# Hash products read in a permuted column order, three VectorE steps put elsewhere, and one more low part in 24 on GpSimd

## The chip, the cores and the metric

The kernel runs on one core of a Trainium2 chip. The metric is the time of one execution in microseconds (us). The engines are called as the profile calls them: PE is TensorE (PEld its weight loads), DVE is VectorE, ACT is ScalarE, POOL is GpSimd, SP is SyncE, which here only issues DMAs.

## The reference

There are 4 x 8 heads of 768 rows with 64 features. A row of q or k gets a hash of 6 bits (the signs of its products with `proj`), and a query attends only to keys with the same hash. The attention output, as 3072 rows of 512, goes through a layer of width 2048 with a piecewise quadratic activation.

```python
q_bits = (np.einsum('bhsd,dk->bhsk', q, proj) > 0)      # the same for k
mask = q_bucket[:, :, :, None] == k_bucket[:, :, None, :]
scores = np.where(mask, scale * q @ k.T, -1e9)
attn = softmax(scores)
x = (attn @ v)  ->  (3072, 512)
h = x @ w_in
g = where(h >= 1, h, where(h <= -1, 0, (h + 1)**2 / 4))
out = g @ w_out
```

## The kernel before

Everything is float32, and products are made from parts: a value is split into a high part (rounded for the matmul) and a low part, and the products of the parts are added up in PSUM. The attention (until about 442 us) runs over 384 units `g`, 12 to a head: two half heads (384 query columns each) of six blocks of 128 keys. Two heads make a pair of 24 units. In the text a unit is numbered 0 to 23 within its pair; units 0 to 11 are the even head, 12 to 23 the odd one. So the half heads of a pair are units 0 to 5, 6 to 11, 12 to 17 (the third half head) and 18 to 23.

Unit `g` is written out in the loop at L691 to L715, and each engine runs its share in that order:

- `s_unit(g)`: two matmuls (L437, L438) put the scores into one of four PSUM banks `s`; ACT writes the high part of the exponential to `ph` (L446) and the whole exponential either back to PSUM or to an SBUF tile `pf` (L451).
- `max_red` (L376): DVE reduces the row maxima whose products were made at the end of the unit before. There is one such pair of matmuls (L359, tile `smax`, one buffer) at the end of every even unit, so the reduction stands at the head of every odd unit, behind the scores.
- `lo_unit(g - 1)`: the low part `pl`, by POOL for key blocks 0 and 3 of a half head (`POOL_J`), by DVE for the other four (both print as L39, the line of `sub`).
- `pv_unit(g - 4)`: three matmuls (L471, L473 with `ph`, L475 with `pl`) add the unit's product with v to the bank `obank[hf]`. `PV_ORDER` says in which order the six blocks of a half head are taken; at the end of a half head ACT copies the bank out (`xs`, L481).
- then the tasks that were registered for unit `g`, in the order in which they were registered.

Three kinds of task matter here.

The hash bits of the pair two ahead: `bits_mm` makes four matmuls (L235) into `obank[1]`, and ACT writes the negated second half of them (`neg`, L241); `bits_cmp` (L246) is a DVE comparison that reads the bank and `neg`. For pairs 4 to 15 the first half is multiplied in unit 5 and compared in unit 6, the second half is multiplied in unit 7, into the same bank, and compared in unit 8. `bits_scale` (L305 on POOL, L303 on ACT for pairs 1 and 2) turns the flags into the values that are put into the operands, and `bits_put` (L314) issues four DMAs for them in unit 18.

The conversion of the weights (`WeightSplit.steps`), one block of 512 columns per head: `rebias` on ACT (L82) and `tail` on DVE (L86, which writes its word into `obank[0]`, free at that point), `shifted` on DVE (L90), `signed` on DVE (L94), which reads that word for the last time. Counted from the head in which the conversion begins they stand in units 9, 10, 11 and 14.

The maxima's way back: POOL clamps them (L403, L405), PE transposes them (L414).

`streamed` and `into` (L42, L47) are two views of eight columns at a time: a matmul that reads `streamed(x)` and writes `into(ps)` takes the eight columns in the order 0 4 1 5 2 6 3 7 and writes them one after the other. L437, L438, L359 and L471 to L475 do so; L235 reads and writes straight.

Of the kernel before, what the change touches and what calls it, by code (L numbers as in the profile page):

```python
# [11 lines left out]
F32 = mybir.dt.float32  # L12
# [10 lines left out]
P = 128  # L23
NH = B * H
NPAIR = NH // 2
NJ = S // P
HS = S // 2
# [14 lines left out]
def streamed(t):  # L42

    return t.rearrange("p (g r w) -> p g w r", r=2, w=4)


def into(t):  # L47
    return t.rearrange("p (g w r) -> p g w r", w=4, r=2)
# [71 lines left out]
NQK, NV, NP_ = 3, 2, 7  # L120
LAG = 4
POOL_J = (0, 3)
PV_ORDER = (1, 2, 0, 4, 5, 3)
NU = 2 * NJ
SHIFT = 4


def attention(ctx, tc, wst, T1, T2, qk, v, pj, cv, x_d, s_d, e_d, tasks, shared):
    nc = tc.nc
    const = ctx.enter_context(tc.tile_pool(name="aconst", bufs=1))  # L130
    work = ctx.enter_context(tc.tile_pool(name="awork", bufs=2))
# [28 lines left out]
    pw = const.tile([P, 3, P], F32R, name="pw")  # L160
# [68 lines left out]
    def bits_mm(pr, hf, bank):  # L229
        t1, t2 = T1[pr % NQK], T2[pr % NQK]  # L230
        sl = slice(hf * HS, (hf + 1) * HS)
        ps = obank[bank]
        for n in range(4):
            h, x = n // 2, (t2[:, 1], t1[:, 0])[n % 2]
            nc.tensor.matmul(out=ps[:, 0:HS], lhsT=pw[:, h, :], rhs=x[:, h, sl], start=(n == 0), stop=(n == 3))  # L235
        if hf == 0:
            bits_t[pr] = (small.tile([32, S], F32R, name="bits", bufs=1),
                          small.tile([32, S], F32, name="neg", bufs=1), {})
        bt, neg, pss = bits_t[pr]
        pss[hf] = ps  # L240
        nc.scalar.activation(out=neg[:, sl], in_=ps[32:64, 0:HS], func=AF.Copy, scale=-1.0)  # L241
# [56 lines left out]
    def bits_scale(pr, eng, hf=None):  # L298
        bt, neg, _ = bits_t[pr]
        if hf is not None:  # L300
            bt, neg = (t[:, hf * HS:(hf + 1) * HS] for t in (bt, neg))
        if eng is nc.scalar:
            eng.activation(out=bt, in_=neg, func=AF.Identity, scale=cvt[:, 0:1], bias=cvt[:, 1:2])  # L303
            return
        eng.tensor_scalar(out=bt, in0=neg, scalar1=cvt[:, 0:1], scalar2=cvt[:, 1:2],  # L305
                          op0=ALU.mult, op1=ALU.add)
# [118 lines left out]
    units = {}  # L425

    def pool_lo(g):
        return g % NJ in POOL_J

    def s_unit(g):  # L430
        hd, hf, j = g // NU, (g % NU) // NJ, g % NJ
        pr, h = hd // 2, hd % 2
        t1, t2 = T1[pr % NQK], T2[pr % NQK]
        sl = slice(hf * HS, (hf + 1) * HS)
        ks = slice(j * P, (j + 1) * P)
        ps = ps_s.tile([P, 512], F32, name="s")
        nc.tensor.matmul(out=into(ps[:, 0:HS]), lhsT=t1[:, 1, h, ks], rhs=streamed(t1[:, 0, h, sl]), start=True, stop=False)  # L437
        nc.tensor.matmul(out=into(ps[:, 0:HS]), lhsT=t2[:, 1, h, ks], rhs=streamed(t2[:, 0, h, sl]), start=False, stop=True)  # L438
        ph, pl = PH[g % NP_], PL[g % NP_]
        if hd >= NH - 2 and j == 4:  # L440
            pf = ps[:, 0:HS]
            nc.scalar.activation(out=pf, in_=pf, func=AF.Exp, scale=SCALE)
            nc.vector.tensor_copy(out=ph[:, 0:HS], in_=pf)
            units[g] = (pf, ph, pl)
            return
        nc.scalar.activation(out=ph[:, 0:HS], in_=ps[:, 0:HS], func=AF.Exp, scale=SCALE)  # L446
        if pool_lo(g):
            pf = work.tile([P, HS], F32, name="pf", bufs=2)
        else:
            pf = ps[:, 0:HS]  # L450
        nc.scalar.activation(out=pf, in_=ps[:, 0:HS], func=AF.Exp, scale=SCALE)  # L451
        units[g] = (pf, ph, pl)
# [7 lines left out]

    def pv_unit(n, between):
        hd, hf, jj = n // NU, (n % NU) // NJ, n % NJ
        j = PV_ORDER[jj]
        pr, h = hd // 2, hd % 2
        va, vb = VA[pr % NV], VB[pr % NV]
        _, ph, pl = units.pop(n - jj + j)
        o = obank[hf]
        w = HS if hf == 0 else HS + 8
        wa = va[:, j, h:h + 2, :].rearrange("p g d -> p (g d)")
        wb = vb[:, j, h:h + 2, :].rearrange("p g d -> p (g d)")  # L470
        nc.tensor.matmul(out=into(o[:, 0:w]), lhsT=wa, rhs=streamed(ph[:, 0:w]), start=(jj == 0), stop=False)  # L471
        between(3)
        nc.tensor.matmul(out=into(o[:, 0:w]), lhsT=wb, rhs=streamed(ph[:, 0:w]), start=False, stop=False)  # L473
        between(4)
        nc.tensor.matmul(out=into(o[:, 0:HS]), lhsT=wa, rhs=streamed(pl), start=False, stop=(jj == NJ - 1))  # L475
        if jj == NJ - 1:
            if hf == 0:
                xss[hd] = work.tile([P, S + 2], F32, name="xs")
            xs = xss[hd]
            w = HS if hf == 0 else HS + 2  # L480
            nc.scalar.copy(out=xs[:, hf * HS:hf * HS + w], in_=o[:, 0:w])  # L481
            if hf == 1:
                xss.pop(hd)
                rs, sr = 64 * h, 64 * (1 - h)
                nc.sync.dma_start(out=x_d[hd // H][rs:rs + 64, pr % (H // 2), :], in_=xs[rs:rs + 64])
                nc.sync.dma_start(out=s_d[hd // H][hd % H:hd % H + 1, :], in_=xs[sr:sr + 1, 0:S])
# [42 lines left out]
    def at(g, fn, *a):  # L529
        tasks[g].append((fn, a))  # L530

    first = [raw0(), raw0()]
    for hf in range(2):
        sl = slice(hf * HS, (hf + 1) * HS)
# [107 lines left out]
    for hd in range(NH):  # L642
        pr, h = hd // 2, hd % 2
        g = hd * NU
        if 0 < hd < NH - 2:
            gc, gt = ((30, 32), (41, 43))[hd - 1] if hd < 3 else (g + NU + SHIFT - 1, g + NU + SHIFT + 1)
            at(gc, max_clamp, hd + 2, nc.gpsimd)
            at(gt, max_tr, hd + 2)
            at(gt, max_put, hd + 2)
        if h == 0 and pr + 2 < NPAIR:  # L650
            g0 = g + (13, 2)[pr] if pr < 2 else g
            for n in range(4):
                gq = g0 + n + (pr == 1 and n == 3)
                at(gq, cast_h, pr + 2, nc.gpsimd, n % 2, n // 2)
                at(gq, low_h, pr + 2, nc.gpsimd, n % 2, n // 2)
            for n in range(2):
                at(g0 + 3 + (pr == 1), move, pr + 2, n)
            at(g0 + 6, move, pr + 2, 2)
            if pr + 3 < NPAIR:
                at(g0 + 7, load_raw, pr + 3)  # L660
            bits_at = (((20, 1), (22, 0)), ((8, 1), (11, 0)))[pr] if pr < 2 else ((5, 1), (7, 1))
            for hf, (n, bank) in enumerate(bits_at):
                at(g + n, bits_mm, pr + 2, hf, bank)
                at(g + n + 1, bits_cmp, pr + 2, hf)
            at(g + n + 1, move, pr + 2, 3)
            if pr:
                at(g + n + 2, bits_scale, pr + 2, nc.gpsimd)
            else:
                at(g + 22, bits_scale, 2, nc.scalar, 0)
                at(g + 24, bits_scale, 2, nc.scalar, 1)  # L670
            at(g + (18 if pr else 24), bits_put, pr + 2)
        if h == 0 and pr + 1 < NPAIR:
            gv = g + LAG + (2 if pr else 16)
            at(gv, cast_v, pr + 1, nc.scalar)
            at(gv + 1, split_v, pr + 1, nc.gpsimd, 0)
            at(gv + 3, split_v, pr + 1, nc.gpsimd, 1)
            if pr + 2 < NPAIR:
                at(gv + (6 if pr else 4), load_v, pr + 2)
# [7 lines left out]
    for i in range(2 * NJ):  # L686
        n = 5 * 31 + 35 * i // 4
# [500 lines left out]
def lsh_attn_ffn(ctx: ExitStack, tc: tile.TileContext, qk, v, pj, cv, w_in, w_out, out):  # L1188
    nc = tc.nc
# [42 lines left out]
    def at(g, fn, *a):  # L1232
        tasks[g].append((fn, a))

    def conv(g, steps, offs):
        for fn, n in zip(steps, offs):
            at(g + n, fn)
# [6 lines left out]
    def wi_steps(i, cp, stage=None):  # L1244
        return ws.steps(win_v[:, :, i * P:(i + 1) * P, :], (P, NCT, P, 2), wih[i], wil[i], cp, stage, None, wq[i], word)
# [4 lines left out]
    woh = [hi for hi, lo in wo]  # L1250
    wol = [lo for hi, lo in wo]
    for i in range(NW1):
        conv((2 * i + 3) * NU, wi_steps(i, nc.scalar), (0, 9, 10, 11, 14 - (i == 0), 17, 19, 21))
    g0 = (NH - 4) * NU
    late = {}
    for n in range(NSTG):
        i = n - (NFT - NW1)
        stage = wq[NW1 + n] if i < 0 else xdp.tile([P, DM], F32, name=f"wd{n}")
        if i < 0:
            first, late[n] = wi_steps(NW1 + n, nc.gpsimd, stage)  # L1260
        elif i < 2:
            first, late[n] = wo_steps(i, nc.gpsimd, stage)
        else:
            first, late[n] = wo_steps(i, nc.scalar, stage, nc.gpsimd if i < 4 else nc.vector)
        conv((4 + 2 * n) * NU, first, (0, 9, 10, 11, 14, 16))
    for n, g in enumerate((1, 7, 13, 25, 30, 35)):
        conv(g0 + g, late[n], (0, 5, 6))

# [1 line left out]
    for b in range(B - 1):  # L1270
        g = (b + 1) * H * NU + LAG + 4
# [32 lines left out]
    for i in range(2, NFT):  # L1304
        n = i + NFT - NW1
# [71 lines left out]
```

## Time and profile before

| | us |
|---|---|
| median of three runs | 926.28 (926.24 to 926.52) |
| the profiled execution, its own time | 929.79 |
| its span, first to last instruction | 927.4 |
| mean granted clock of PE | 0.997 |

The profile comes from one execution of its own, 3.5 us longer than the median; 2.4 us of its time lie outside the span. In the views a matmul is shown with its whole duration (326 ns for 384 columns), though the next one starts after about half of that, so a busy PE is not a PE that never waits. What PE loses is seen from the starts of its instructions in the timeline, and from what the weight load ahead of a matmul waited for (PEld in the list of waits). DVE and ACT instructions overlap the next one of their engine by some 0.1 us as well, so sums of durations can pass the length of a stretch.

### The profile page before, as it was taken

Reading aid. Unit: us, or ns where it says so; the run is one execution under the profiler, and the core shown is the slowest. Engines: PE = TensorE matmul, PEld = TensorE weight load, DVE = VectorE, ACT = ScalarE, POOL = GpSimd, SP = SyncE. Lnnn points to the kernel's source line nnn. Section 1 sums busy time; section 2 is a strip of 40 time slices with the busy share of each in tenths; the row PEclk is TensorE's granted clock in tenths of the full one; section 3 lists DMA queues with packets and bytes.
Section 4 is the critical chain, followed back from the end, with each engine's and each line's share of the span. In section 5 each row is a group of like instructions: output and inputs, shape, how many; then the busy total and the mean of one; then the engine's idle time right before and its main releaser. Section 6 shows DMA issues by size and latency. Waiting matters only on the chain.

```text
span 927.4 us, 15714 instructions
## 1 busy us (share of the span) xinstructions
PE 906.7 (98%) x5050; PEld 846.2 (91%) x5050; DVE 753.1 (81%) x1345; ACT 669.6 (72%) x1481; POOL 320.8 (35%) x428
## 2 busy tenths in 40 slices
PE   8999999999999999999999999999999999999997
PEld 7789999999999999999999998989999999999996
DVE  8878889988998899887798888788876778765564
ACT  7889998999989998998766565556565555554454
POOL 8867766667777666678100000000000000000000
PEclk9999999999999999999999999999999999999999
DMA  6776666776656666654496478976549564454431
GB/s 162 187 189 162 166 187 179 202 209 186 185 159 176 183 183 195 146 153 131 142 316 210 131 255 297 296 252 193 160 148 272 152 202 126 145 179 128 125 91 69
DMA packets 95691, 167.67 MB, mean 181 GB/s; under 512 B 14533, under 2 KB 52537, under 8 KB 95609
## 3 DMA queue, kind: packets, MB, share of 16 engines
q1 hardware_dynamic: 95344, 166.63, 62.4%
q8 instruction: 40, 0.66, 0.3%
q14 instruction: 43, 0.34, 0.1%
q10 hardware_dynamic: 264, 0.03, 0.0%
HBM read 106.13 MB, written 33.96 MB: 151 GB/s over the span
## 4 chain that ended last, share of the span: by engine, by line
PE 70%; ACT 10%; DMA 5%; DVE 5%; POOL 3%; issue 2%; SPq 1%; ACTq 0%; DVEq 0%; POOLq 0%
PE y L911 24%; PE h L1143 16%; PE h L1048 6%; PE smax L359 4%; PE s L437 4%; PE s L438 3%; PE o L475 3%; PE o L471 3%; PE o L473 3%; ACT ph L446 3%; ACT s L451 2%; PE o L235 2%; DVE nm L376 2%; DMA t<-bits 2%; DMA wq<-wsq 1%
## 5 line engine op out<-in xcount | busy, mean ns | idle before, releaser
L446 ACT ACTIVATE ph<-s 128x384 fp32r<-128x384 f32 x380 | 191.7, 504 | 32.6 <-PE s L438 30.7
L376 DVE TENSOR_REDUCE nm<-smax 128x1 f32<-128x768 f32 x168 | 159.7, 950 | 10.7 <-PE smax L359 9.1
L39 DVE TENSOR_TENSOR pl<-s,ph 128x384 fp32r<-128x384 f32 x256 | 137.8, 549 | 24.7 <-ACT s L451 19.3
L39 POOL TENSOR_TENSOR pl<-pf,ph 128x384 fp32r<-128x384 f32 x128 | 129.7, 1014 | 78.9 <-ACT pf L451 72.2
L876 DVE SCALAR_TENSOR_TENSOR t<-t 128x384 f32<-128x384 f32 x128 | 71.3, 557 | 87.3 <-ACT z L871 87.0
L451 ACT ACTIVATE s<-s 128x384 f32<-128x384 f32 x252 | 128.8, 511 | 0.0
L471 PE MATMUL o<-ph,va 128*128 128x392 f32 (+1 forms) x384 | 126.0, 328 | 0.7 <-DVE neg L246 0.7
L437 PE MATMUL s<-t 128*128 128x384 f32 x384 | 126.3, 329 | 0.0
L475 PE MATMUL o<-pl,va 128*128 128x384 f32 x384 | 125.4, 327 | 0.4 <-DVE pl L39 0.4
L473 PE MATMUL o<-ph,vb 128*128 128x392 f32 (+1 forms) x384 | 125.8, 328 | 0.0
L438 PE MATMUL s<-t 128*128 128x384 f32 x384 | 125.3, 326 | 0.1
L911 PE MATMUL y<-t,ghi 128*128 128x512 f32 x384 | 118.7, 381 | 2.0 <-ACT ghi L881 2.0
L359 PE MATMUL smax<-t 128*128 128x384 f32 x336 | 87.0, 341 | 6.0 <-DVE nm L376 4.3
L881 ACT CAST ghi<-z 128x384 fp32r<-128x384 f32 x129 | 64.9, 503 | 31.8 <-DVE z L877 31.4
L871 ACT ACTIVATE z<-t,m 128x384 f32<-128x384 f32 x128 | 78.7, 615 | 4.2
L911 PEld LDWEIGHTS y<-t,ghi 128*128 128x128 f32 x384 | 71.5, 190 | 8.8 <-ACT ghi L881 2.6
L1143 PE MATMUL h<-wbig,t 128*128 128x384 f32 x399 | 77.5, 329 | 0.3 <-DVE wsq L1162 0.3
L877 DVE TENSOR_TENSOR z<-t,z 128x384 f32<-128x384 f32 x128 | 71.4, 558 | 4.5
L911 PE MATMUL y<-woh,glo 128*128 128x512 f32 x192 | 73.1, 381 | 0.8 <-DVE glo L885 0.8
L870 ACT ACTIVATE t<-h,mh 128x384 f32<-128x384 f32 x56 | 32.5, 580 | 57.1 <-PE h L1048 33.7
L437 PEld LDWEIGHTS s<-t 128*128 128x128 f32 x384 | 72.5, 189 | 1.2
L475 PEld LDWEIGHTS o<-pl,va 128*128 128x128 f32 x384 | 72.6, 189 | 1.1 <-DVE pl L39 0.7
(207 smaller groups left out, 2029.8 us busy)
## 6 DMA issues: line engine op xcount, KB each, us to landing
t<-wc SPq DMA_DIRECT2D x92, 256.0 KB
t<-t SPq DMA_DIRECT2D x60, 384.0 KB
wraw<-wc SPq DMA_DIRECT2D x76, 256.0 KB
raw<-in_qk_dram SPq DMA_DIRECT2D x14, 768.0 KB
wraw<-in_w_in_dram SPq DMA_DIRECT2D x16, 512.0 KB
wraw<-in_w_out_dram SPq DMA_DIRECT2D x16, 512.0 KB
t<-ed SPq DMA_DIRECT2D x36, 192.0 KB
xd<-xs SPq DMA_DIRECT2D x32, 192.5 KB
```

The source lines that it names most:

```text
L39: eng.tensor_tensor(out=out, in0=a, in1=b, op=ALU.subtract)
L359: nc.tensor.matmul(out=into(ps[:, 0:HS]), lhsT=t2[:, 0, h, i * P:(i + 1) * P], rhs=streamed(t2[:, 1, h, hf * HS:(hf + 1) * HS]), start=Tru ...
L376: nc.vector.tensor_reduce(out=nmp(hd)[:, i:i + 1], in_=smax[hd][:, :, 0:HS], axis=AX.XY, op=ALU.max, negate=True)
L437: nc.tensor.matmul(out=into(ps[:, 0:HS]), lhsT=t1[:, 1, h, ks], rhs=streamed(t1[:, 0, h, sl]), start=True, stop=False)
L438: nc.tensor.matmul(out=into(ps[:, 0:HS]), lhsT=t2[:, 1, h, ks], rhs=streamed(t2[:, 0, h, sl]), start=False, stop=True)
L446: nc.scalar.activation(out=ph[:, 0:HS], in_=ps[:, 0:HS], func=AF.Exp, scale=SCALE)
L451: nc.scalar.activation(out=pf, in_=ps[:, 0:HS], func=AF.Exp, scale=SCALE)
L471: nc.tensor.matmul(out=into(o[:, 0:w]), lhsT=wa, rhs=streamed(ph[:, 0:w]), start=(jj == 0), stop=False)
L473: nc.tensor.matmul(out=into(o[:, 0:w]), lhsT=wb, rhs=streamed(ph[:, 0:w]), start=False, stop=False)
L475: nc.tensor.matmul(out=into(o[:, 0:HS]), lhsT=wa, rhs=streamed(pl), start=False, stop=(jj == NJ - 1))
L911: nc.tensor.matmul(out=into(ys[c][m]), lhsT=g_[:, m * P:(m + 1) * P], rhs=streamed(w), start=(first and k == 0), stop=(last and k == 2))
L1143: nc.tensor.matmul(out=into(ps), lhsT=w[:, cs], rhs=streamed(x), start=(n == 0 and s not in (2, 3, 6)), stop=(n == 5), skip_group_check=True)
```

## The change

It has six parts.

1. The hash products (L235) read `streamed` columns and write `into` the bank, so that the flags stand in permuted order; `bits_scale` puts them back: it reads `into(neg)` and writes `streamed(bt)`, with a step of four elements in what it writes.
2. For pairs 4 to 15, the first hash comparison is registered for unit 7 and no longer for unit 6. In unit 7 it stands behind that unit's reduction on DVE, and ahead of the second half's products on PE.
3. `signed` is registered one unit earlier (13 for 14), but for one block of `w_in` that keeps 14 and one that had 13. There it stands behind unit 13's or unit 1's reduction and ahead of the low part that it followed.
4. In the third half head of pairs 2 to 14 the low part of key block 5 goes to POOL too (`QUARTER_J`).
5. From unit 48 on (pair 2) the blocks of a half head are taken in the order 1 0 2 4 3 5 (`PV_LATER`).
6. `pf` has three buffers for two.

```diff
 POOL_J = (0, 3)
+FROM = 4 * 12
+QUARTER_J = ((0, 3), (0, 3), (0, 3, 5), (0, 3))
 PV_ORDER = (1, 2, 0, 4, 5, 3)
+PV_LATER = (1, 0, 2, 4, 3, 5)
 NU = 2 * NJ
...
         for n in range(4):
             h, x = n // 2, (t2[:, 1], t1[:, 0])[n % 2]
-            nc.tensor.matmul(out=ps[:, 0:HS], lhsT=pw[:, h, :], rhs=x[:, h, sl], start=(n == 0), stop=(n == 3))
+            nc.tensor.matmul(out=into(ps[:, 0:HS]), lhsT=pw[:, h, :], rhs=streamed(x[:, h, sl]), start=(n == 0),
+                             stop=(n == 3))
...
             bt, neg = (t[:, hf * HS:(hf + 1) * HS] for t in (bt, neg))
+        bt, neg = streamed(bt), into(neg)
         if eng is nc.scalar:
...
     def pool_lo(g):
-        return g % NJ in POOL_J
+        return g % NJ in (QUARTER_J[g // NJ % 4] if FROM <= g < (NH - 2) * NU else POOL_J)
...
         if pool_lo(g):
-            pf = work.tile([P, HS], F32, name="pf", bufs=2)
+            pf = work.tile([P, HS], F32, name="pf", bufs=3)
...
-        j = PV_ORDER[jj]
+        j = (PV_LATER if n >= FROM else PV_ORDER)[jj]
...
             for hf, (n, bank) in enumerate(bits_at):
                 at(g + n, bits_mm, pr + 2, hf, bank)
-                at(g + n + 1, bits_cmp, pr + 2, hf)
+                at(g + n + 1 + (pr > 1 and hf == 0), bits_cmp, pr + 2, hf)
...
     for i in range(NW1):
-        conv((2 * i + 3) * NU, wi_steps(i, nc.scalar), (0, 9, 10, 11, 14 - (i == 0), 17, 19, 21))
+        conv((2 * i + 3) * NU, wi_steps(i, nc.scalar), (0, 9, 10, 11, 14 if i == 1 else 13, 17, 19, 21))
...
-        conv((4 + 2 * n) * NU, first, (0, 9, 10, 11, 14, 16))
+        conv((4 + 2 * n) * NU, first, (0, 9, 10, 11, 13, 16))
```

## Rows read from the trace of the kernel before

**Rows 1.** The head of the page and its first part: the span, and the busy time of each engine with its share of the span and its instructions.

```profile
span 927.4 us, 15714 instructions
PE 906.7 (98%) x5050; PEld 846.2 (91%) x5050; DVE 753.1 (81%) x1345; ACT 669.6 (72%) x1481; POOL 320.8 (35%) x428
```

**Rows 2.** Busy time by stretch, for the even head of pair 7 (units 0 to 11) and its odd head (units 12 to 23): length, busy us of PE, PEld, DVE, ACT and POOL (instructions), granted clock, DMA share, GB/s.

```profile
206.90:220.70 13.80, 13.66 (x82) 13.01 (x82) 11.92 (x20) 13.04 (x32) 12.64 (x17) 1.00 0.56 134
220.70:233.20 12.50, 12.28 (x75) 11.73 (x74) 11.49 (x18) 11.32 (x30) 6.09 (x9) 1.00 0.81 242
```

**Rows 3.** Who waited for whom in the whole span: us in total, times, longest us.

```profile
PEld smax L359 <- DVE nm L376: 14.7, 30, 0.6
...
DVE neg L246 <- ACT neg L241: 6.7, 13, 0.6
...
PE smax L359 <- DVE nm L376: 4.3, 18, 0.3
```

**Rows 4.** Timeline of PE from unit 5 to unit 8 of pair 7: start, us, line, tile and count. Both lines of L235 are hash products.

```profile
213.43 0.92 PE L235 MATMUL o<-t,pw 128*128 128x384 f32 x4
214.18 0.32 PE L437 MATMUL s<-t 128*128 128x384 f32 x1
...
214.99 0.49 PE L359 MATMUL smax<-t 128*128 128x384 f32 x2
215.32 0.33 PE L437 MATMUL s<-t 128*128 128x384 f32 x1
...
216.13 0.87 PE L235 MATMUL o<-t,pw 128*128 128x384 f32 x4
216.84 0.32 PE L437 MATMUL s<-t 128*128 128x384 f32 x1
```

**Rows 5.** Timeline of DVE from unit 6 to unit 15 of pair 7. L246 is the first hash comparison, L376 the reductions of units 7, 11, 13 and 15, L86 `tail`, L94 `signed`; L39 is the low part of unit 13.

```profile
215.00 0.55 DVE L246 TENSOR_TENSOR neg<-o,neg 32x384 f32<-32x384 f32 x1 [0.53 <-ACT neg L241]
215.52 0.96 DVE L376 TENSOR_REDUCE nm<-smax 128x1 f32<-128x768 f32 x1
...
219.94 0.70 DVE L86 TENSOR_SCALAR o<-wraw 128x512 int32<-128x512 int32 x1 [0.16 <-ACT xs L481]
220.54 0.95 DVE L376 TENSOR_REDUCE nm<-smax 128x1 f32<-128x768 f32 x1
...
223.00 0.95 DVE L376 TENSOR_REDUCE nm<-smax 128x1 f32<-128x768 f32 x1
223.86 0.55 DVE L39 TENSOR_TENSOR pl<-s,ph 128x384 fp32r<-128x384 f32 x1
224.33 0.74 DVE L94 SCALAR_TENSOR_TENSOR wsq<-wsq,wsc,o 128x512 int32<-128x512 int32 x1
224.98 0.95 DVE L376 TENSOR_REDUCE nm<-smax 128x1 f32<-128x768 f32 x1
```

**Rows 6.** Timeline of PE at unit 14 (three lines) and at unit 2 (the last line) of pair 7, at the matmuls of the maxima.

```profile
223.46 0.33 PE L475 MATMUL o<-pl,va 128*128 128x384 f32 x1
224.00 0.59 PE L359 MATMUL smax<-t 128*128 128x384 f32 x2 [0.22 <-DVE nm L376]
224.43 0.33 PE L437 MATMUL s<-t 128*128 128x384 f32 x1
...
209.96 0.59 PE L359 MATMUL smax<-t 128*128 128x384 f32 x2
```

**Rows 7.** Timeline of ACT in units 7 to 9 of pair 7: the second `neg`, and the scores and the copy of the bank `xs` at the end of unit 9.

```profile
217.38 0.48 ACT L241 ACTIVATE neg<-o 32x384 f32<-32x384 f32 x1
...
218.68 0.48 ACT L446 ACTIVATE ph<-s 128x384 fp32r<-128x384 f32 x1
219.05 0.49 ACT L451 ACTIVATE pf<-s 128x384 f32<-128x384 f32 x1
219.42 0.49 ACT L481 COPY xs<-o 128x384 f32<-128x384 f32 x1
```

**Rows 8.** All of line L235 in the span: count, then duration in ns (least, median, most), first and last start.

```profile
L235 PE MATMUL o<-t,pw x120: 331/337/444, 21.6 to 375.8; 128*128 128x384 f32 x120
```

**Rows 9.** Timeline of POOL in units 9 to 12 of pair 7: the scaling of the hash bits, and the low part of unit 9.

```profile
219.15 0.98 POOL L305 TENSOR_SCALAR bits<-neg,cvt 32x768 fp32r<-32x768 f32 x1
...
221.06 1.00 POOL L39 TENSOR_TENSOR pl<-pf,ph 128x384 fp32r<-128x384 f32 x1
```

**Rows 10.** Timeline of DVE in units 17 to 19 of pair 7: the low parts of units 16 and 17, and the reduction of unit 19.

```profile
227.49 1.01 DVE L39 TENSOR_TENSOR pl<-s,ph 128x384 fp32r<-128x384 f32 x2
228.68 0.96 DVE L376 TENSOR_REDUCE nm<-smax 128x1 f32<-128x768 f32 x1 [0.17 <-PE smax L359]
```

**Rows 11.** The last two heads: timeline of PE at 422 us, of POOL at the low parts of units 378 and 381, and of PE at the products of the last half head.

```profile
422.84 0.43 PE L475 MATMUL o<-pl,va 128*128 128x384 f32 x1 [0.37 <-DVE pl L39]
...
437.37 1.99 POOL L39 TENSOR_TENSOR pl<-pf,ph 128x384 fp32r<-128x384 f32 x2
...
437.77 0.33 PE L475 MATMUL o<-pl,va 128*128 128x384 f32 x1
...
438.44 0.43 PE L475 MATMUL o<-pl,va 128*128 128x384 f32 x1
```

**Rows 12.** Busy time by stretch, after the attention (columns as in the second group).

```profile
574.00:577.00 3.00, 1.26 (x7) 0.83 (x5) 1.58 (x3) 1.79 (x4) 0.00 (x0) 1.00 1.04 364
578.00:579.00 1.00, 1.00 (x4) 1.00 (x4) 0.58 (x2) 1.00 (x3) 0.00 (x0) 0.50 1.03 307
```

## The prediction

> **What bounds the kernel now.** I read the page's busy times first, then two stretches of one pair, then the list of waits, then the timelines. PE is busy 98% of the span [rows 1], and in both heads of pair 7 it leaves 0.14 to 0.22 us idle [rows 2]. But matmuls overlap, so the starts say more. The five matmuls from 214.18 to 214.99 take 0.81 us, 0.162 each [rows 4]: that is PE's pace for 384 columns, and wherever the next start comes later, PE lost time. The list of waits shows to whom: 14.7 + 4.3 us went to maxima products that waited for DVE's reduction of the maxima before them [rows 3]. In pair 7 one such place is unit 14: L475 starts at 223.46, the two maxima products follow at 224.00 where they were due at 223.62, and with them PE is held until 224.43 where an undisturbed pair takes 0.33 us, as from 214.99 to 215.32; so 0.48 us are lost [rows 4, 6]. Unit 2 has the same shape, with 0.59 us for the two matmuls [rows 6]. So in the attention PE sets the pace, and DVE's bursts take some tenths of a us from it twice in a pair. After the attention the change touches nothing.
>
> DVE's burst: from `tail` at 219.94 to the end of unit 13's reduction at 223.95 DVE never waits; `tail` itself had waited for `xs` on ACT [rows 5]. DVE is no bound of the whole: it waited 0.53 us for ACT ahead of the first hash comparison [rows 5], 6.7 us over 13 comparisons [rows 3].
>
> **The first comparison** is the part that decides. Before, it runs at 215.00 to 215.55, and the second half's products, which write the same bank, come at 216.13 [rows 4, 5]: 0.58 us to spare. After, it stands behind unit 7's reduction. That starts at 215.52, right when the maxima products of unit 6 are through (second one at 215.15 plus 0.33), so it can't be earlier. The next DVE instruction starts 0.86 us after a reduction, as 223.00 to 223.86 shows, so the comparison starts at 216.38 and ends at 216.92 [rows 5]. Queued behind it on PE are the four products of the second half, and behind those in turn units 8 and on: PE takes nothing past them. At unit 14 DVE ends at 223.95, PE starts at 224.00 (0.05 later), and the restarted pair takes 0.10 more than an undisturbed one (0.43 against 0.33) [rows 5, 6]. So PE resumes at 216.97 for 216.13, and loses 0.84 + 0.10 = 0.94 us. This happens for pairs 4 to 15, 12 times: **+11.3 us**; without the restart 10.1.
>
> What DVE wins by it: nothing, since the reduction that it lets ahead started as soon as PE had its input, and the 0.53 us of waiting had no work to fill them.
>
> **What is handed back.** A PE that is later lets ACT and DVE catch up, so a later DVE stall shrinks. The chain is ACT's second `neg`, the scores of units 8 and 9, `xs`, `tail`, reduction. ACT takes 2.04 us from the second `neg` at 217.38 to `xs` at 219.42 [rows 7]. After the change the second products begin at 216.97 and end at about 217.90, so `neg` starts at 217.94; with nothing to wait for, `xs` starts at 219.98. But unit 9's scores, 0.9 us later than now, hold ACT for about 0.16, so I take 220.14. Moved with PE it would be 220.32: 0.18 earlier by this count, 0.34 without that wait. `tail` and the reductions of units 11 and 13 come earlier by the same, and the stall at unit 14 shrinks from 0.48 to about 0.30. The bounds are 0 and the whole of it with 0.09 that unit 12 loses, 0.57. I take 0.18, worked out from the rows nearest to it: **-2.2 us** for 12 pairs (0 to -6.8).
>
> **The order of columns.** The second group of four hash products takes 0.71 us from 216.13 to 216.84, 0.176 each, against 0.162 for the streamed ones [rows 4]. There are 120 [rows 8]: 120 x 0.0135 = **-1.6 us** (-1.2 to -1.8, by how the first of each group counts). Here a rule speaks against the change. The Trainium skill, Advanced Engine Details and Errata, section Memory Cachelines, says that SBUF reads reach full speed when following accesses stay within a line of 16 bytes, and pay when each goes to another line; 0 4 1 5 in float32 changes the line each time. By that rule the order should cost, but the trace disagrees: 0.162 against 0.176. It is a rival below all the same.
>
> **The scale step** writes with a step of four elements, which no row shows. On POOL it takes 0.98 us now and could take from 0.98 to double. Behind it stand a part of v and unit 9's low part, which ends at 222.06 [rows 9]. By the new order that is wanted by the L475 at 223.46 [rows 6], which itself moves 0.7 later, so 2.1 us cover it. I take 0. On ACT (four times, early pairs) I take 0, at most +1.
>
> **The other orders.** POOL's additional low part (13 times) takes 0.55 us off DVE [rows 10], but DVE then waits 0.17 us for PE's next maxima: PE gains 0. It runs on POOL in the odd head, where POOL is busy 6.1 of 12.5 us [rows 2]; if that cover went, a late low part would hold PE by up to its own 1.0 us. `signed` at unit 13 changes places with the low part of unit 13. Both lie between two reductions that DVE reaches without a pause (223.00, 223.86, 224.33, 224.98) [rows 5], so the sum is the same: 0. The low part is 0.65 us later (224.33 to 224.98 is what `signed` takes), and the products of unit 16 want it, two units on, or ten matmuls of 0.162: 1.6 us. The word's bank comes free 0.5 us sooner, which nobody waits for. The third `pf` costs and saves nothing: no wait for one is in the list.
>
> `PV_LATER` gives DVE's low parts more time and POOL's less. In pairs 2 to 13 the smallest margin left for POOL is the 1.4 us of unit 9. In the last two heads it is otherwise: it removes the wait for DVE at 422.84 (0.37 us idle) and asks for unit 378's low part at 437.77, while POOL delivers at about 438.39 in a row without gaps; before, it was wanted only at 438.26 and PE went on at 438.44 [rows 11]. Since POOL sets the time there, the gain at 422 us is spent waiting, and one more unit of 0.49 us is left behind the wait: between -0.6 and +0.5, I take **+0.3**.
>
> **Sum:** 11.3 - 2.2 - 1.6 + 0.3 = +7.8 us. On the profile's own 929.79 (span 927.4 and 2.4 around it) that is 937.6; on the median of 926.28 it is **934.1**. The profiled execution is 3.5 longer than the median, but nothing in the sum hangs on it.
>
> **The rivals.**
>
> *The comparison's wait isn't there* (the change doesn't do what it says): the second products come after it anyway, or don't wait. For: only the order of registration says that they must. Against: they write the bank that it reads. Then 926.28 - 1.6 + 0.3 = 925.0, perhaps less.
>
> *DVE's relief gives all back*, the case that ends not slower: 13 low parts off DVE are 7.1 us, `signed` is earlier, and PE's pause at unit 7 lets DVE come out of its burst before unit 14. For: 19.0 us of waits on reductions [rows 3], about 1.2 us a pair. Against: the burst begins with `tail` at 219.94, behind the gifts, and DVE was idle just before. It decides in units 10 to 14 and 22 to 2: from 0.8 us given back per pair there is no loss left. If all 1.2 came back, 12 x (0.94 - 1.2) - 1.6 = -4.7: 921.6; between, about 926.
>
> *The permuted read costs*, by the rule above: as a mechanism of this kernel, the hash products become slower by what they should gain: +1.6 for -1.6, 937.3.
>
> *The clock falls*: after PE stood still for most of 574 to 577 us (busy 1.26 of 3.00) the granted clock was 0.50, the 1.2 GHz level, at 578 [rows 12]. A stall of 0.94 is between that and the 0.48 that did nothing at unit 14. If each of 12 stalls brought some 3 us at that level, +18 us: 952.
>
> **How the numbers follow.** Forecast 0.80, no wait 0.08, all given back 0.06, permuted read 0.04, clock 0.02. The ends of the unknown costs give 10.1 - 6.8 - 1.8 - 0.6 = +0.9 and 11.3 - 1.2 + 0.5 + 1.0 = +11.6, so 927.2 to 937.9; what lies outside is the no-wait case, most of the case of all given back, and the clock, under 2 in 10. The measurement of this kernel can tell about 0.2% (1.9 us) from no change. Slower by more: 0.80 + 0.04 + 0.02 = 0.86; within: 0.06, all given back; faster: 0.08.
>
> **What would show it.** The timeline of PE at unit 7 must show the second hash products some 0.9 us behind the L475 before them, the list of waits a new row of about 10 us, L235 waiting for DVE `neg` L246, 12 times; the wait of DVE for ACT `neg` must be nearly gone. L235 should have a median near 326 ns. The stall at unit 14 should be near 0.3 us, that at unit 2 unchanged. In the last head PE should wait for POOL's low part. I am wrong if L235 starts without a gap, or if the waits on reductions fall by 10 us.

## The result and the profile after

The changed kernel takes 935.99 us (median; 935.12 to 936.40), the kernel before 926.39 (926.24 to 926.52) beside it: ratio 1.0102, 95% interval 1.0085 to 1.0120, so 9.6 us slower. The forecast was 934.1 in a range of 927.2 to 937.9.

The two profiles are only 7.2 us apart. The attention itself is 9.0 us longer: its last product with v starts at 448.99 for 440.03. What follows took 485.6 us in the profile after and 487.4 in the one before, where the granted clock was 0.50 from 577.8 to 581.2.

The profile after, first the span and the busy times as in [rows 1]:

```profile
span 934.6 us, 15897 instructions
PE 906.5 (97%) x5050; PEld 843.7 (90%) x5050; DVE 748.0 (80%) x1332; ACT 672.7 (72%) x1481; POOL 342.7 (37%) x441
```

PE and DVE do no more than before; the 13 low parts have gone from DVE's 1345 instructions to POOL's 428. What has grown is PE's standing still, and the list of waits (us in total, times, longest us) says for whom; the kernel's lines are moved by three to five, so L238 are the hash products, L245 `neg`, L250 the comparison, L364 and L381 the maxima and their reduction, L480 the product with `pl`:

```profile
PEld smax L364 <- DVE nm L381: 12.6, 28, 0.6
PEld o L238 <- DVE neg L250: 11.8, 12, 1.0
...
DVE neg L250 <- ACT neg L245: 5.7, 13, 0.6
...
PE smax L364 <- DVE nm L381: 1.1, 4, 0.3
```

The second of these lines is one that the kernel before did not have: the weight load of the hash products waits 12 times, once for the bits of each of the pairs 4 to 15 (made in pairs 2 to 13), 11.8 us in all. The waits for the reductions are 12.6 + 1.1 = 13.7 us for 19.0. In pair 7 PE's timeline shows unit 7 (first three lines), unit 12 and unit 14 (last three):

```profile
219.77 0.33 PE L480 MATMUL o<-pl,va 128*128 128x384 f32 x1
220.79 0.92 PE L238 MATMUL o<-t,pw 128*128 128x384 f32 x4 [0.69 <-DVE neg L250]
221.54 0.33 PE L442 MATMUL s<-t 128*128 128x384 f32 x1
...
226.27 0.49 PE L364 MATMUL smax<-t 128*128 128x384 f32 x2
...
228.07 0.33 PE L480 MATMUL o<-pl,va 128*128 128x384 f32 x1
228.53 0.59 PE L364 MATMUL smax<-t 128*128 128x384 f32 x2
228.96 0.33 PE L442 MATMUL s<-t 128*128 128x384 f32 x1
```

At unit 7 the four hash products should have followed the L480 after 0.162 us, at 219.93, and taken 0.65, so that L442 started at 220.58. It starts at 221.54: 0.96 us lost, of which 0.86 stand ahead of the first product and 0.10 in the restart (0.75 for 0.65). Unit 12's maxima take an undisturbed 0.49, and unit 14 now loses 0.40 (228.96 for 228.07 + 0.16 + 0.33), where it lost 0.48 in [rows 6].

DVE's timeline of the same units, as in [rows 5]:

```profile
219.32 0.96 DVE L381 TENSOR_REDUCE nm<-smax 128x1 f32<-128x768 f32 x1 [1.01 <-PE smax L364]
220.19 0.54 DVE L250 TENSOR_TENSOR neg<-o,neg 32x384 f32<-32x384 f32 x1
...
222.25 0.55 DVE L250 TENSOR_TENSOR neg<-o,neg 32x384 f32<-32x384 f32 x1 [0.42 <-ACT neg L245]
...
227.53 0.94 DVE L381 TENSOR_REDUCE nm<-smax 128x1 f32<-128x768 f32 x1
228.40 0.73 DVE L94 SCALAR_TENSOR_TENSOR wsq<-wsq,wsc,o 128x512 int32<-128x512 int32 x1
229.05 0.55 DVE L39 TENSOR_TENSOR pl<-s,ph 128x384 fp32r<-128x384 f32 x1
229.52 0.94 DVE L381 TENSOR_REDUCE nm<-smax 128x1 f32<-128x768 f32 x1
```

The comparison starts 0.87 after the reduction and ends at 220.73; PE starts 0.06 later. The reduction itself did not start sooner than it would have: DVE now idles 1.01 us ahead of it. The first comparison waits for ACT's `neg` no more, but the second one, at 222.25, now does, because its products come late; so that row of the list has hardly shrunk (5.7 us for 6.7). `signed` and the low part have changed places between two reductions that stand 1.99 us apart, as before (1.98).

The hash products have the streamed pace, but the steps that put the order back have become long (all of a line: ns least, median, most). POOL's step took 0.98 us before [rows 9]; ACT's, the last line here, is from the kernel before:

```profile
L238 PE MATMUL o<-t,pw x120: 326/326/431, 21.8 to 384.6; 128*128 128x384 f32 x120
```

```profile
L310 POOL TENSOR_SCALAR bits<-neg,cvt x13: 1756/1762/1772, 65.2 to 386.2; 32x768 fp32r<-32x768 f32 x13
L308 ACT ACTIVATE bits<-neg,cvt x4: 1078/1081/1084, 26.2 to 48.1; 32x384 fp32r<-32x384 f32 x4
```

```profile
L303 ACT ACTIVATE bits<-neg,cvt x4: 687/692/702, 26.0 to 47.5; 32x384 fp32r<-32x384 f32 x4
```

### The profile page after: what moved, and what is told of

Its sections match the earlier page's. It is cut to its first block, busy times and chain, and to the rows that moved or that the text cites. A ratio compares the mean times of both kernels' runs of the same rounds, so it can differ in the third digit from the quotient of the medians.

```text
span 934.6 us, 15897 instructions
## 1 busy us (share of the span) xinstructions
PE 906.5 (97%) x5050; PEld 843.7 (90%) x5050; DVE 748.0 (80%) x1332; ACT 672.7 (72%) x1481; POOL 342.7 (37%) x441
## 4 chain that ended last, share of the span: by engine, by line
PE 56%; ACT 17%; DVE 9%; DMA 9%; issue 5%; POOL 2%; SPq 1%; ACTq 0%; DVEq 0%; POOLq 0%
PE y L916 22%; PE h L1148 15%; ACT ph L451 6%; PE h L1053 5%; ACT s L456 3%; ACT pf L456 2%; PE smax L364 2%; DMA t<-bits 2%; DMA wraw<-in_w_in_dram 2%; DVE nm L381 2%; PE s L443 2%; PE s L442 2%; PE o L480 1%; PE o L476 1%; PE o L478 1%
## 5 line engine op out<-in xcount | busy, mean ns | idle before, releaser
L381 DVE TENSOR_REDUCE nm<-smax 128x1 f32<-128x768 f32 x168 | 159.7, 950 | 28.3 <-PE smax L364 25.8
L39 POOL TENSOR_TENSOR pl<-pf,ph 128x384 fp32r<-128x384 f32 x141 | 142.8, 1017 | 64.0 <-ACT pf L456 55.3
L39 DVE TENSOR_TENSOR pl<-s,ph 128x384 fp32r<-128x384 f32 x243 | 131.5, 548 | 21.5 <-POOL pl L39 9.7
L442 PE MATMUL s<-t 128*128 128x384 f32 x384 | 126.4, 329 | 0.0
L480 PE MATMUL o<-pl,va 128*128 128x384 f32 x384 | 125.5, 327 | 0.3 <-POOL pl L39 0.3
L456 ACT ACTIVATE s<-s 128x384 f32<-128x384 f32 x239 | 121.4, 508 | 0.0
L364 PE MATMUL smax<-t 128*128 128x384 f32 x336 | 86.0, 338 | 4.4 <-DVE nm L381 1.1
L442 PEld LDWEIGHTS s<-t 128*128 128x128 f32 x384 | 72.6, 189 | 1.3
L480 PEld LDWEIGHTS o<-pl,va 128*128 128x128 f32 x384 | 72.6, 189 | 1.0 <-POOL pl L39 0.9
L443 PEld LDWEIGHTS s<-t 128*128 128x128 f32 x384 | 72.6, 189 | 0.5 <-DMA t<-te 0.5
```

Source lines behind the costliest of these rows:

```text
L39: eng.tensor_tensor(out=out, in0=a, in1=b, op=ALU.subtract)
L364: nc.tensor.matmul(out=into(ps[:, 0:HS]), lhsT=t2[:, 0, h, i * P:(i + 1) * P], rhs=streamed(t2[:, 1, h, hf * HS:(hf + 1) * HS]), start=Tru ...
L381: nc.vector.tensor_reduce(out=nmp(hd)[:, i:i + 1], in_=smax[hd][:, :, 0:HS], axis=AX.XY, op=ALU.max, negate=True)
```

## The experiments

Theory W: PE waits at the second hash products for the first comparison, because both use one bank and the comparison stands behind a reduction. Rival S: the scale step in permuted order costs the time. Rival O: the comparison's new place on DVE costs by itself. Later theories are named where they come up. The length of a pair is the time from the first score product of pair 7 to that of pair 8, in PE's timeline; before it is 26.33 us (206.88 to 233.21). PE's timeline before, with unit 12 between the two starts:

```profile
206.88 0.33 PE L437 MATMUL s<-t 128*128 128x384 f32 x1
...
221.40 0.33 PE L475 MATMUL o<-pl,va 128*128 128x384 f32 x1
221.57 0.58 PE L359 MATMUL smax<-t 128*128 128x384 f32 x2
221.98 0.33 PE L437 MATMUL s<-t 128*128 128x384 f32 x1
...
233.21 0.33 PE L437 MATMUL s<-t 128*128 128x384 f32 x1
```

At unit 12, 0.58 us pass from L475 to the score product where 0.16 + 0.33 are due: 0.09 lost.

**The comparison alone.**

```diff
-                at(g + n + 1, bits_cmp, pr + 2, hf)
+                at(g + n + 1 + (pr > 1 and hf == 0), bits_cmp, pr + 2, hf)
```

> The kernel before with part 2 alone: the first hash comparison of pairs 4 to 15 stands behind unit 7's reduction. Theory W (PE waits at the second hash products for that comparison): 12 waits of 0.96 us, of which about 0.16 each comes back at units 12 and 14, so +9.6 us, 936.0; the list of waits shows some 11 us of the products' weight loads waiting for DVE neg. Theory S (the loss comes from the scale step, which on POOL took 1.76 us in the changed kernel and 0.98 before): no loss without the permuted order, 926.4. Theory O (it is the comparison's place on DVE that costs, whatever PE does): slower too, but without PE's wait.

Measured 935.88 us against 926.33, ratio 1.0101 (1.0087 to 1.0115): the whole loss from this one line, without any permuted order. The wait is there as in the changed kernel, and the pair takes 27.14 us; first the list of waits, then the timeline's starts of pairs 7 and 8:

```profile
PEld o L235 <- DVE neg L246: 11.8, 12, 1.0
```

```profile
210.34 0.33 PE L437 MATMUL s<-t 128*128 128x384 f32 x1
...
237.48 0.33 PE L437 MATMUL s<-t 128*128 128x384 f32 x1
```

In the changed kernel these starts are 27.02 apart, 0.12 less, and that is the streamed hash products:

```profile
210.72 0.33 PE L442 MATMUL s<-t 128*128 128x384 f32 x1
...
237.74 0.33 PE L442 MATMUL s<-t 128*128 128x384 f32 x1
```

**The change without it.** The same line put back in the changed kernel.

> The changed kernel with part 2 alone undone. Theory W: all of the loss goes, and what is left is the gain of the streamed hash products (120 x 0.0135 = 1.6 us) against some 0.3 to 0.8 us at the start and in the last two heads: 925.5, between 924.8 and 926.4. Theory S: still about 935. Stall at unit 14 again 0.49 us and at unit 12 0.08 us under W.

Measured 926.94, ratio 1.0005 (0.9996 to 1.0014); the wait is gone, and S falls. But 926.94 lies above the expected range (924.8 to 926.4): the gain of the streamed products isn't there.

**The streamed products alone**, part 1 in the kernel before.

> The kernel before with part 1 alone: hash products streamed, the scale step puts the order back. Theory W with the sizes of the prediction: -1.6 us, less up to 0.4 at the start, where four scale steps on ACT take 1.08 us for 0.69: 925.0. Theory S: +8 us or more, 934, with a wait behind the scale step on POOL or behind the operands that it feeds. Hash products at a median of 326 ns under both.

Measured 927.03, ratio 1.0006 (0.9997 to 1.0015): no loss of S's size, and no gain. The pair is 26.32 us long, as before, though eight products take 0.11 less. PE's timeline at unit 12 shows where that went:

```profile
221.20 0.33 PE L477 MATMUL o<-pl,va 128*128 128x384 f32 x1
221.45 0.59 PE L361 MATMUL smax<-t 128*128 128x384 f32 x2
221.88 0.33 PE L439 MATMUL s<-t 128*128 128x384 f32 x1
```

From L477 to the score product behind the maxima 0.68 us pass, where 0.16 + 0.33 = 0.49 are due: 0.19 lost, and 0.09 before. PE comes sooner and waits longer. Who sets the time is seen in ACT's timeline, from the second `neg` to `xs`:

```profile
217.28 0.48 ACT L242 ACTIVATE neg<-o 32x384 f32<-32x384 f32 x1
...
219.31 0.49 ACT L483 COPY xs<-o 128x384 f32<-128x384 f32 x1
```

2.03 us, as the 2.04 in [rows 7]: ACT works from unit 5 to `xs` with hardly a pause, `tail` waits for `xs`, and DVE's burst behind `tail` sets unit 14. This became theory A: in the kernel before ACT paces units 5 to 14, and what PE saves there is lost. (At the start, pair 0 also became longer, 32.85 us for 32.22; it has three of the four long scale steps on ACT.)

**Another bank for the second half.** The comparison stays behind the reduction, and the products don't write the bank that it reads.

```diff
-        ps = obank[bank]
+        ps = obank[bank] if bank is not None else ps_s.tile([P, 512], F32, name="s")
...
-            bits_at = (...)[pr] if pr < 2 else ((5, 1), (7, 1))
+            bits_at = (...)[pr] if pr < 2 else ((5, 1), (7, None))
```

> The changed kernel, but the second half's hash products of pairs 4 to 15 go into one of the four score banks, so that they don't write the bank that the first comparison reads; the comparison stays behind unit 7's reduction. Theory W (it is the bank that PE waits for): the wait of 0.96 us at unit 7 is gone and the time is that of the kernel without part 2, 925.5, up to 1 us more if the score banks become short. Theory O (the comparison's place on DVE costs by itself): still about 935.

Measured 927.85, ratio 1.0017 (1.0008 to 1.0025). L238 waits for DVE `neg` no more, and the pair is back at 26.33 us (206.98 to 233.31). So it is the bank that PE waits for, and O falls; the 0.9 us above the kernel without part 2 is within what was allowed for the score banks. Where they arise is not known: in the profiles the attention is no longer (last product with v at 440.7 for 440.9).

**The order of the blocks alone**, part 5, and **parts 3, 4 and 6 alone.**

> The kernel before with part 5 alone (order 1 0 2 4 3 5 from unit 48 on). As predicted: nothing in pairs 2 to 13, and in the last two heads the wait for DVE at the third product goes while the waits for POOL's low parts grow by some 0.5 us; pair 14 is 0.2 us shorter in the changed kernel. So +0.3 us, 926.6. Rival: the order frees DVE's tightest low parts and PE gains at units 2 and 14: 916 to 922.

> The kernel before with parts 3, 4 and 6 alone: signed one unit earlier, key block 5 of the third half head on POOL, three buffers of pf. As predicted: 0, 926.4, with the stalls at units 2, 12 and 14 unchanged (0.41, 0.08, 0.49 us), since DVE's burst begins with tail, behind both. Rival: 13 x 0.55 = 7.1 us less DVE work shortens the pairs, 920 or less.

Measured 926.81 against 927.12 (0.9998; 0.9989 to 1.0007) and 926.12 against 927.12 (0.9992; 0.9983 to 1.0001). Neither can be told from no change, and pair 7 stays at 26.32 in both. DVE's 7.1 us of relief don't shorten the pairs; only pair 14 is 0.2 shorter with it (24.35 for 24.58).

**`tail` early, its word in SBUF.** A try at DVE's burst itself.

```diff
-        return ws.steps(..., cp, stage, None, wq[i], word)
+        return ws.steps(..., cp, stage, None, wq[i], None)
...
-        conv((2 * i + 3) * NU, wi_steps(i, nc.scalar), (0, 9, 10, 11, 14 - (i == 0), 17, 19, 21))
+        conv((2 * i + 3) * NU, wi_steps(i, nc.scalar), (0, 9, 7, 11, 14 - (i == 0), 17, 19, 21))
```

and the same two edits for the staged blocks.

> The kernel before with tail three units earlier (offset 7 for 10), its word in SBUF and not in the bank that ACT's copy xs frees. A test of what stalls PE at units 2, 12 and 14: if it is DVE's burst that begins with tail behind xs, 0.6 us less in it takes 0.08 + 0.49 us away in the even head's end and 0.41 at the pair's beginning, so up to 12 x 0.97 = 11.6 us: 915, between 914 and 919. If PE's wait comes from somewhere else (the reduction itself, or ACT): 926, and if SBUF words slow DVE or POOL down: above that.

Measured 938.96, ratio 1.0133 (1.0117 to 1.0148): slower, the third of the cases expected. With the word in SBUF `signed` takes 1.53 us at unit 2, where POOL works beside it, and 0.73 at unit 14, where POOL has nothing to do. DVE's timeline at both places of pair 7, and POOL's at unit 2:

```profile
215.12 1.53 DVE L94 SCALAR_TENSOR_TENSOR wsq<-wsq,wsc,wa 128x512 int32<-128x512 int32 x1
...
230.13 0.73 DVE L94 SCALAR_TENSOR_TENSOR wsq<-wsq,wsc,wa 128x512 int32<-128x512 int32 x1
```

```profile
215.10 1.00 POOL L39 TENSOR_TENSOR t<-raw,t 128x384 fp32r<-128x384 f32 x1
216.04 0.97 POOL L177 CAST t<-raw 128x384 fp32r<-128x384 f32 x1
```

In the kernel before `signed` takes 0.74 [rows 5]. Behind the long `signed` PE loses 0.82 us at unit 4, where it lost nothing before; unit 14 loses 0.88 for 0.48, and ahead of it `tail` (0.91 us for 0.70) and `shifted` (1.00 for 0.75) are longer too. The run changed two things at once, so it doesn't say what the earlier `tail` alone is worth.

**The same, with the transposes a unit later** (`g + NU + SHIFT + 2` for `+ 1`).

> As the kernel with the early tail, and the transpose of the maxima stands in unit 6 (and 18) for unit 5 (and 17), so that POOL's clamp is done when PE comes to it. The wait at unit 5 is 0.25 us in the kernel before, of which 0.05 follow the short weight load in any case. 12 x 0.2 = 2.4 us less than the kernel with the early tail if that wait is on the path; 0 if ACT or DVE take it back in the next units, as they did with the 0.1 us of the streamed products.

Measured 937.50, ratio 1.0116 (1.0102 to 1.0130), 1.5 us below the run before on the same chip, where 2.4 or 0 was expected. The wait at unit 5 can't be the reason: in pair 7 of the run before the transpose followed its product after 0.16 us, without a wait. What came back stands mainly at unit 14 (0.76 lost for 0.88); why is open.

**v's cast in the odd head.** For theory A: less ACT work in units 5 to 9 (POOL's two low parts of v move with it).

```diff
-            gv = g + LAG + (2 if pr else 16)
+            gv = g + LAG + (12 if 2 <= pr <= 12 else 2 if pr else 16)
```

> The kernel before with ACT's cast of v (0.83 us) and POOL's two low parts of v (1.0 us each) moved from the even head (from unit 6) to the odd head (from unit 16), for pairs 2 to 12. A test of what paces units 5 to 14. Theory A (ACT, which works without a pause from unit 5 to the copy xs at the end of unit 9, sets when DVE's burst begins): xs and tail come up to 0.8 us sooner against PE, the stalls at units 12 and 14 (0.08 and 0.49 us) shrink to below 0.2 together, and 11 pairs give 4 to 6 us: 921 to 923. Rival B (DVE alone sets the pace): the stalls stay, 926.5.

Measured 925.80 against 927.02, ratio 0.9986 (0.9977 to 0.9995). The pair takes 26.23 us (206.49 to 232.72), 0.10 less than before. PE's timeline at unit 14:

```profile
223.00 0.33 PE L475 MATMUL o<-pl,va 128*128 128x384 f32 x1
223.46 0.59 PE L359 MATMUL smax<-t 128*128 128x384 f32 x2
223.89 0.33 PE L437 MATMUL s<-t 128*128 128x384 f32 x1
```

0.40 us are still lost, exactly as in the changed kernel; unit 12 loses nothing, and 0.06 are lost anew at unit 20. ACT is no longer behind, for its second `neg` waits for PE:

```profile
216.66 0.48 ACT L241 ACTIVATE neg<-o 32x384 f32<-32x384 f32 x1 [0.32 <-PE o L235]
```

So A was right in kind and too large in size: ACT's lateness is worth 0.08 at unit 14 and 0.09 at unit 12. The other 0.40 I put down to the chain from PE's unit 9 over `xs`, `tail` and DVE's six instructions, which moves with PE; that they stay the same whether PE pauses at unit 7 or not speaks for it, but no run cut that chain alone.

**And streamed products with it**, from pair 4 on.

> As the kernel with v's cast moved, and the hash products of pairs 4 to 15 streamed (with the scale step that puts the order back, on POOL). Theory A: with ACT no longer in the way the 8 x 0.0135 = 0.11 us of a pair stay won, unlike in the kernel with the streamed products alone, where they came back as a longer stall at unit 12: 12 x 0.11 = 1.3 us below the kernel with v's cast moved. Rival B: no difference to that kernel.

Measured 924.94, ratio 0.9975 (0.9967 to 0.9984), against 925.80 for the run before: 0.9 less where 1.3 was expected. The pair takes 26.11 us (205.82 to 231.93), 0.12 less again: now the eight products' 0.11 stay won. Pair 0 stays at 32.22, without the long steps on ACT. This version beats both kernels, the one before by 2.1 us.

**The odd head's conversion in units 16 to 20.**

```diff
-        conv((2 * i + 3) * NU, wi_steps(i, nc.scalar), (0, 9, 10, 11, 14 - (i == 0), 17, 19, 21))
+        conv((2 * i + 3) * NU, wi_steps(i, nc.scalar), (0, 4, 5, 7, 8, 17, 19, 21))
```

with the word of these blocks in `obank[1]`.

> The kernel before with the conversion of the blocks that begins in the odd head drawn forward into units 16 to 20 (rebias, tail, shifted, signed at offsets 4, 5, 7, 8 for 9, 10, 11, 14), its word in the other bank, which no hash product uses in the odd head. If the stall at unit 2 (0.41 us) comes from DVE's burst of tail and shifted at units 22 and 23, it goes: 12 x 0.41 = 4.9 us, 921.5, up to 3 us less gain if DVE's load in units 16 to 20 makes new stalls there. If it comes from elsewhere: 926.5 or above.

Measured 967.24, ratio 1.0434 (1.0413 to 1.0455). The stall at unit 2 is gone, as a line of PE's timeline shows (0.49 for the 0.59 of [rows 6]):

```profile
227.08 0.49 PE L359 MATMUL smax<-t 128*128 128x384 f32 x2
```

PE stands still elsewhere in these pairs, so this alone proves little. But the kernel before has the same at unit 2 of pair 14, which has no conversion in the head ahead of it:

```profile
395.11 0.49 PE L359 MATMUL smax<-t 128*128 128x384 f32 x2
```

So the stall does come from `tail` and `shifted` at units 22 and 23. The time is lost because `rebias` now comes before its load has landed, 12 times, 32.4 us in all, and ACT holds the scores up meanwhile:

```profile
247.97 0.67 ACT L82 ACTIVATE wsq<-wraw 128x512 f32<-128x512 f32 x1 [3.88 <-DMA wraw<-in_w_in_dram]
```

Behind four of these pauses PE also ran at the 1.2 GHz level, 17 us in all; in pair 7 no matmul started between 246.17 and 249.62, and then (length, busy us of PE, PEld, DVE, ACT and POOL, granted clock, DMA share, GB/s):

```profile
250.70:254.00 3.30, 3.10 (x11) 3.10 (x11) 3.26 (x6) 2.46 (x6) 1.17 (x2) 0.50 0.14 23
```

There the score products follow each other after 0.32 us for 0.16, so by my estimate the clock costs up to half of the 17 us.

**The same with the load ten units ahead**, v's cast in unit 18 and streamed products.

> The kernel with v's cast in the odd head (now unit 18) and streamed hash products, and the odd head's conversion in units 16 to 20 as tried before, but with its load issued ten units ahead of rebias, six more than in that run, where ACT waited for the load and held the scores up. The stall at unit 2 was gone there. If that is DVE's burst and nothing else, it stays gone and 12 x 0.41 = 4.9 us come off the 924.9 of the kernel with v's cast and streamed products: 920, up to 2 us more if DVE's load in units 16 to 20 makes smaller stalls. If the load still comes late, or DVE pays in the odd head what it saves: 925 or above.

Measured 973.39, ratio 1.0500 (1.0476 to 1.0524). The load is in time. The mean granted clock is 0.982 here, and ACT now waits for another transfer, 11 times, 43.0 us in all: that of a block's earlier result out of `wsq`, of which there are two buffers:

```profile
253.45 0.66 ACT L82 ACTIVATE wsq<-wraw 128x512 f32<-128x512 f32 x1 [3.48 <-DMA wq<-wsq]
```

Whether the 4.9 us of unit 2 can be had is open: it would take an earlier store of that result, or a third buffer. Neither was tried.

## Why the prediction was right, and where its sizes were off

**The wait**, 12 x 0.94 = 11.3 us: measured 0.96 each, 11.5. Its parts hold one by one (the comparison 0.87 behind a reduction, 0.06 to PE, 0.10 for the restart). That PE waits, and for the bank, is shown by the comparison alone and by the other bank.

**What is handed back**, 12 x 0.18: measured 0.17, made of 0.09 at unit 12 and 0.08 at unit 14. The size came out, the place only in half: the stall at unit 14 is 0.40 and not about 0.30, since PE, no longer held at unit 12, comes there sooner. The upper bound of 0.57 was much too wide, and the run with v's cast moved says why: only ACT's lateness can be caught up; the other 0.40 of unit 14 stay.

**The streamed products**, -1.6 us, were booked as a gain that hangs on nothing else, and that is the step that was wrong. They gain nothing alone (927.03 against 926.33, +0.7 with an interval of -0.3 to +1.4), since unit 12's wait takes their 0.11 a pair back. In the changed kernel PE's pause has taken that wait away, so they do give 0.12 a pair (27.14 to 27.02), 1.3 for 12 pairs, what the sum has for 96 of the 120 products; that this term came out there is luck. And the changed kernel and the comparison alone have the same time (935.99 and 935.88), so the 1.3 is spent at the ends of the attention. In these two profiles pair 0 takes 0.3 more with the long steps on ACT (32.51 for 32.21), for which I had taken 0 and at most 1, pair 1 takes 0.5 more (29.23 for 28.75; without any change to it this pair varies by as much between runs), and the last two heads 0.5 more, while pair 14 takes 0.2 less.

**The last two heads**, +0.3: from pair 15's first score product to the last product with v 23.63 us, 23.12 before, so +0.5, the upper bound; the order of the blocks alone has 23.53. That the sum still has +0.3 here is luck: pair 14 is 0.2 shorter, by the low part on POOL, which had been taken as 0. The wait for POOL's low part is where it was forecast, one product earlier; PE's timeline and then POOL's:

```profile
446.91 0.43 PE L480 MATMUL o<-pl,va 128*128 128x384 f32 x1 [0.16 <-POOL pl L39]
```

```profile
445.84 1.99 POOL L39 TENSOR_TENSOR pl<-pf,ph 128x384 fp32r<-128x384 f32 x2
```

**The terms taken as 0** (part 4, `signed`, the third `pf`) were 0 in their own run but for these 0.2. The scale step on POOL became 0.8 us longer, within the bounds (up to double), and its cover held: unit 9's low part ends at 226.56, and the product that wants it is the L480 at 228.07.

**The sum:** pairs 2 to 13 are 0.69 longer each, 8.3 us (27.02 for 26.33); with 0.4 ahead of them and 0.3 behind that is 9.0 of the 9.6 measured. What is left seems to lie behind the attention, where the change touches nothing: the 485.6 us there compare with 484.2 to 485.0 in the profiles of the twelve experiments. Why is open.

**The signs.** Two of those named did not come: the stall at unit 14 near 0.3 (0.40), and DVE's wait for ACT's `neg` nearly gone (5.7 us for 6.7); the prediction had followed the first comparison only, and the second took over its wait. The others came, the new row of 11.8 us and the 326 ns among them.

**The rivals.** That the wait isn't there: no. That DVE's relief gives all back: no, parts 3, 4 and 6 alone changed nothing, and the case needed 0.8 a pair where 0.17 came. That the permuted read costs: no, 326 ns for 337; the rule of the Trainium skill on lines of 16 bytes (Advanced Engine Details and Errata, Memory Cachelines) does not hold for these reads. That the clock falls: no, the mean granted clock after is 1.000, so the 12 pauses of 0.96 us did not bring what four of the longer pauses brought in the run with the odd head's conversion moved.

## What to carry to other kernels

Ask of every step that is moved behind another not only what it gives way to, but which buffer it holds meanwhile and whose next write stands in line for that buffer: here one line made PE, the engine that sets the pace, wait for a comparison of 0.54 us behind a reduction of 0.96, and that reduction had not been late. A saving on the busiest engine is worth nothing in a stretch where its next wait is set by a chain through other engines: look whether the wait behind it grows by what was saved. And taking load off an engine helps only at the place where that engine is late; 7.1 us off DVE, taken where it was idle anyway, gave nothing that could be measured.

## What the runs showed of the hardware

Putting the columns back cost POOL and ACT more busy time than reading them permuted saved PE (13 x 0.78 + 4 x 0.39 = 11.7 us for 120 x 0.0135 = 1.6): with a step of four elements in what it writes, POOL's scale step of 32 x 768 took 1.76 us for 0.98, ACT's of 32 x 384 1.08 for 0.69.

A DVE instruction with two inputs in SBUF can take twice its time beside POOL: with its word in SBUF `signed` took 1.53 us at unit 2, and it ended at 216.65, 0.55 after the POOL instruction (215.10 to 216.10) that had started just ahead of it. POOL's next one, the cast at 216.04, took 0.97 us for 0.51 elsewhere in the same pair. At unit 14, with no POOL instruction beside it, `signed` took 0.73 with the same word, and in the kernel before, with the word in PSUM, its durations in the attention lay between 735 and 741 ns, beside POOL or not. The Trainium skill has this as a rule (SBUF — State Buffer, Who interferes with whom): such an instruction shares a read port with a GpSimd instruction that reads SBUF, and the later one is blocked until the other is through. The trace agrees: the long `signed` ends behind the POOL instruction that started 0.02 us ahead of it.
